# Attention and a feed-forward network on one core: pairs of units from unit 16 on, other slots for them, and the transposes' copy moved ahead of the exponentials

## The chip, the core and the metric

The kernel runs on one core of a Trainium2 chip. TensorE multiplies matrices into PSUM, VectorE and ScalarE do elementwise work, GpSimd a little more, and SP issues nearly all transfers. The metric is device time of one launch in microseconds; lower is better. The time before is 655.12 us, the median of 3 runs (654.51 to 655.52).

## The reference

Banded attention with a few global keys, then a two-layer network on its output.

```
scores = q @ k^T / sqrt(D);  rel = i - j;  keep = (j < 8) | ((rel >= 0) & (rel < 96))
bias   = -slope[h] * (96 where the key is global and not local, else |rel|)
a      = softmax(where(keep, scores + bias, -1e9));  x = a @ v        # float32
h = x @ w_in;  g = max(0.01 * h, h);  out = g @ w_out
batch 4, heads 8, seq 768, head_dim 64; 3072 tokens, d_model 512, d_ff 2048
```

The weights come as 64-bit floats. The kernel splits each weight and each activation of the network into a high and a low part and forms three of the four products.

## The kernel before

**Units and events.** A unit is one block of 128 queries and four heads; there are 24 blocks with two units each, 0 to 47. A unit passes through three events. In `event(t)` (L345), unit t gets its scores on TensorE (L181), its bias and row minimum on VectorE (`biased`, L195), its exponentials on ScalarE (`exps`, L210) and the reciprocals of its sums (`sums`). Unit t-1 is transposed, and unit t-2 is multiplied with its values (`attn_v`, L314 and L326); the result goes to `xh` on ScalarE (L339) and `xl` on VectorE (L343), the input of the network.

**Two ways to transpose.** Units below `BY_DVE` = 14 are transposed by TensorE: `transposes` (L274) multiplies the exponentials by a diagonal of reciprocals that GpSimd forms (`dg`, L245), and ScalarE copies the result out of PSUM (`keep_pt`, L289), in `event` as the last step but the `x` copies of the lead. Units from 14 on are scaled (L237) and transposed in 32x32 blocks (L240) by VectorE; `move` then writes them to device memory (`via`, L220) and reads them back in four transfers (`pt`, L222).

**Tall units.** `tall(u)` holds for units below 14 that are not in the first block of a sequence. Their near values are laid out so that one matmul contracts over all 128 rows (L326, 8 matmuls of 128x64), where others use 16 matmuls on quarters of the array. The layout of the values in memory (`layout`) follows the same test.

**The lead and the slots.** The eight events 0 to 7 (`LEAD` = 6, `LEAD + 2` events) come first, without the network. Then the network runs in 128 slots. Chunks have 3 blocks, so 384 tokens and six units; a slot does one sixteenth of the hidden layer for one chunk: 12 matmuls into `ps_h` (`ffn1`, L797 to L799), and 9 matmuls of the slot before it into the output (`ffn2`, L818 to L820). The order is: 7 slots of chunk 0 (0 to 6), the 16 of chunk 1 (7 to 22), the other 9 of chunk 0 (23 to 31), then chunks 2 to 7 with 16 slots each (chunk 2 from slot 32). In a slot the events of that slot come first, then `ffn1` of the slot, then `ffn2` of the one before. After a chunk's last `ffn2` its three output tiles are copied out of PSUM (L466, L468) and sent.

**Conversions.** The weights come in 32 pieces (`w_in` and `w_out` in turn). A conversion of one has a scaling on ScalarE (L560), three integer steps on VectorE (L563, L565, L569), a cast on ScalarE (L573) and a subtraction on VectorE (L576). The cast and the subtraction wait in the list `due` for the next `end()` or event. Slot f needs piece 2f, and the slot after it piece 2f+1. Each conversion also issues the load of a later piece. `conv_at` gives the pieces of a slot; conversion 7 runs between event 7 and slot 0.

**Pairs.** From unit `PAIRS` = 22 on, `visit(t)` takes two units at once: `attn_v` of t-2 and t-1, scores of t and t+1, loads, bias. The exponentials of t are done there. Those of t+1, and both `sums` (scaling, transposing and moving), are put in the list `behind`, of which each slot takes one entry at `end()` and one at `more()`, two places inside `ffn1`:

```
behind.extend([lambda: exps(t + 1, [0]), lambda: (exps(t + 1, [1]), sums(t)), lambda: None, lambda: sums(t + 1)])
```

**Order.** TensorE's matmuls are all kept in program order. On the other engines `pin` keeps program order up to slot 22, in slots with a pair and while `behind` is not empty; elsewhere a planner places the instructions. `ev_at` says which event stands in which slot: before, events 8 to 13 in slots 1 to 6; 14 to 19 in slots 23, 25, 26, 28, 29, 31; 20 and 21 in 32 and 35; the pairs 22 and 24 in 39 and 44; then three pairs per chunk, in its slots 2, 7 and 12.

Of the kernel before, what the change touches and what calls it, by code (L numbers as in the profile page):

```python
# [19 lines left out]
D = 64  # L20
NU = 2
BY_DVE = 14
PAIRS = 22
TB = 32
G = 32
WIN = 96
# [3 lines left out]
CHUNKS = [3] * 8  # L30
LEAD_CONV = 7
# [16 lines left out]
def fast_path(ctx, tc, qp, kp, vp, wi, wo, nvec, weights, nmall, out, B, H, S):  # L48
    nc = tc.nc
    NB = S // P  # L50
    DM = H * D
    NK = DM // P
    NF = wi.shape[0]
# [40 lines left out]
    def load_piece(p):  # L94
        if p < len(pieces):
            m, f = pieces[p]
            t = raw.tile([P, NK * P], I64, tag="stage", name="wst", bufs=STAGES)
            pin(nc.sync.dma_start(out=t, in_=(wi, wo)[m][f].rearrange("p a b -> p (a b)")))
            staged[p] = t

    due = []

    def conversion(p):

        m, f = pieces[p]
        dh, dl = ((wih[:, :, f * P:(f + 1) * P], wil[:, :, f * P:(f + 1) * P]), (woh[:, f, :], wol[:, f, :]))[m]
        for n in range(p + 2 + (p > LEAD_CONV - 2), p + 3 + (p > LEAD_CONV - 3)):
            load_piece(n)
        scale, shift, low, *parts = split_float64(tc, pin, att, staged.pop(p), dh, dl)
        due.extend(parts)  # L110
        return scale, shift, low
# [3 lines left out]
    LEAD = NU * CHUNKS[0]  # L115

    def where(u):
        s, uu = divmod(u, NU)
        return s, uu, s % NB
# [45 lines left out]

    def tall(u):

        return u < BY_DVE and where(u)[2] > 0

    def scores(u, av):  # L170
        d = units[u]
# [28 lines left out]
    def exps(u, pairs=range(2)):  # L200
        d = units[u]
        s, uu, i = where(u)
        pr, nm = d["pr"], d["nm"]
        if "sm" not in d:
            d["sm"] = att.tile([P, 4], F32, name="sm", bufs=3)
        sm = d["sm"]
        for a in pairs:
            for j in range(2):
                p = head(u, pr, a, j)
                pin(nc.scalar.activation(out=p, in_=p, func=AF.Exp, scale=-1.0,  # L210
                                         bias=nm[:, 2 * a + j:2 * a + j + 1], accum_out=sm[:, 2 * a + j:2 * a + j + 1]))
# [67 lines left out]
    def keep_pt(u):  # L279
        d = units[u]  # L280
        if u >= BY_DVE:
            return
        s, uu, i = where(u)
        ps = d.pop("ps")
        pt = att.tile([P, 6, 2, HALF], F32, name="pt", bufs=1)
        dst = pt.rearrange("p g f q -> p f g q")
        src = ps[:, :, :6 * HALF].rearrange("p f (g q) -> p f g q", g=6)
        if i:
            pin(nc.scalar.copy(out=dst, in_=src))  # L289
        else:  # L290
            for j in range(2):
                g = slice(3 * j + 1, 3 * j + 3)
                pin(nc.scalar.copy(out=dst[:, :, g], in_=src[:, :, g]))
        d["pt"] = pt
# [43 lines left out]
    def high_x(u, av):  # L338
        pin(nc.scalar.copy(out=parts(u, 0), in_=av[:, :, 2 * KW:]))  # L339
# [5 lines left out]
    def event(t, conv=()):  # L345

        now, mid, old = t < NUNIT, t - 1 in units, t - 2 in units
        if t < LEAD + 2:

            av = (ps_lead if t % 2 else ps_x).tile([P, 2, 512], F32, tag="ps_av", name="ps_sc")  # L350
            scores(t, av)
            if mid and t <= LEAD:
                transposes(t - 1)
            if old:
                ov = ps_lead.tile([P, 2, 512], F32, tag="ps_ov", name="ps_ov")
                attn_v(t - 2, ov)
            if t > LEAD:

                transposes(t - 1)
        else:  # L360

            ov = av = ps_x.tile([P, 2, 512], F32, tag="ps_av", name="ps_av")
            attn_v(t - 2, ov)
            if now:
                scores(t, av)
            if mid:
                transposes(t - 1)
            high_x(t - 2, ov)
        if t + 2 < NUNIT:
            load_qk(t + 2)  # L370
        if t == 0:
            load_piece(1)
        ends = due[:]
        due.clear()
        if ends:
            ends[0]()
        scale, shift, low = conversion(conv[0]) if conv else [lambda: None] * 3
        if t + 1 < NUNIT:
            load_v(t + 1)
        scale()  # L380
        if now:
            biased(t, av)
            if t == LEAD + 1:
                high_x(t - 2, ov)
            exps(t)
        if t > LEAD:
            low_x(t - 2, ov)
        if ends:
            ends[1]()
        shift()  # L390
        if now:
            sums(t)
        low()
        if mid:
            keep_pt(t - 1)
        if old and t <= LEAD:
            high_x(t - 2, ov)
        if old and t <= LEAD:
            low_x(t - 2, ov)

# [26 lines left out]
    half = 7  # L427
# [42 lines left out]
            nc.sync.dma_start(out=out[r0:r0 + P, :], in_=ob)  # L470


    conv_at = {n: [n + LEAD_CONV + 1] for n in range(half)}
    conv_at.update(spread(range(15, 19), range(half, half + 4)))
    conv_at.update(spread(range(19, 2 * NF), range(half + 4, half + NF - 1)))
    ev_at = {}
    for c in range(1, NCHUNK):
        events = range(NU * first_step[c] + 2, NU * first_step[c + 1] + 2)
        slots = (range(1, half) if c == 1 else [23, 25, 26, 28, 29, 31] if c == 2 else [33, 35, 37, 40, 42, 44] if c == 3
                 else range((c - 1) * NF, c * NF - 2))  # L480
        if c > 3:

            events, slots = events[::2], [(c - 1) * NF + s for s in (2, 7, 12)]
        elif c == 3:
            events, slots = [20, 21, 22, 24], [2 * NF + s for s in (0, 3, 7, 12)]
        ev_at.update(spread(events, slots))

    for t in range(2):
# [10 lines left out]
                scale_bias(tc, tabs[:, 1], nbw, H, 1)  # L499
    ps_h = ctx.enter_context(tc.tile_pool(name="ps_h", bufs=1, space=bass.MemoryType.PSUM))  # L500
    ps_o = ctx.enter_context(tc.tile_pool(name="ps_o", bufs=3, space=bass.MemoryType.PSUM))

    for step in (*due, *conversion(LEAD_CONV)):
        if step in due:
            due.remove(step)
        step()
    behind = []
    for j in range(len(order) + 1):
        pinned[0] = j < half + NF or bool(behind) or any(t >= PAIRS for t in ev_at.get(j, ()))
        conv = list(conv_at.get(j, ()))  # L510
        for t in ev_at.get(j, ()):
            if t >= PAIRS:
                visit(t, behind)
# [326 lines left out]
def layout(q, k, v, wi, wo, ng, nl):  # L840
    B, H, S, _ = q.shape
    NB = S // P

    NU_ = H // 4

    ar = np.arange(P)
    near = np.stack([np.where(ar < G, ar - P, ar), np.where(ar < G, ar - P, np.where(ar < HALF, ar + HALF, ar + P))])
    start = (np.arange(NB) - 1)[:, None, None] * P
    own = np.broadcast_to(start + P + ar[:HALF], (NB, 2, HALF))
    near = np.where(ar < G, ar, np.maximum(start + near, 0))  # L850

    qp = q.reshape(B, NU_, 2, 2, NB, P, D).transpose(0, 4, 3, 6, 1, 2, 5)
    qp = np.ascontiguousarray(qp).reshape(B * NB, 2 * D, 2 * NU_, P)

    kh = k.reshape(B, NU_, 2, 2, S, D)
    kp = kh[:, :, :, :, np.concatenate([near, own], 2)]
    kp = np.ascontiguousarray(kp.transpose(0, 4, 1, 3, 7, 2, 5, 6)).reshape(B * NB, NU_, 2 * D, 2, 2, KW)

    kd = kp[BY_DVE // NU:].reshape(-1, NU_, 2 * D, 2, 2, 3, 2, TB).transpose(0, 1, 2, 3, 4, 6, 5, 7)
    kp[BY_DVE // NU:] = kd.reshape(-1, NU_, 2 * D, 2, 2, KW)  # L860

    vh = v.reshape(B, NU_, 2, 2, S, D)
    vn = vh[:, :, :, :, near.reshape(NB, 2, 2, HALF)].transpose(0, 4, 1, 2, 7, 5, 6, 3, 8).reshape(B * NB, NU_, P, 4, 2, D)
    vo = vh[:, :, :, :, own[:, 0]].transpose(0, 4, 1, 2, 5, 3, 6).reshape(B * NB, NU_, P, 1, 2, D)
    vp = np.ascontiguousarray(np.concatenate([vn, vo], 3))

    vt = vh[:, :, :, :, near].transpose(0, 4, 1, 6, 3, 2, 5, 7).reshape(B * NB, NU_, P, 4, 2, D)
    pe = [s for s in range(BY_DVE // NU) if s % NB]
    vp[pe, :, :, :4] = vt[pe]
    DM, DF = wi.shape  # L870
    NJ = DF // P
    wip = np.ascontiguousarray(wi.reshape(DM // P, P, NJ, DF // NJ).transpose(2, 1, 0, 3))
    wop = np.ascontiguousarray(wo.reshape(NJ, DF // NJ // P, P, DM).transpose(0, 2, 1, 3))
    wip, wop = wip.view(np.int64), wop.view(np.int64)
    n = np.concatenate([np.asarray(ng, np.int64).reshape(1), np.asarray(nl, np.int64).reshape(1)]).view(np.int32).reshape(1, 4)
    qt, kt = (np.ascontiguousarray(x.transpose(0, 1, 3, 2)) for x in (q, k))
    vt = np.ascontiguousarray(v.reshape(B, H, NB, P, D).transpose(0, 1, 3, 2, 4))
    return dict(qt=qt, kt=kt, vt=vt, qp=qp, kp=kp, vp=vp, wi=wip, wo=wop, ngl=n)
# [18 lines left out]
```

## Time and profile before

| | |
|---|---|
| median of 3 runs | 655.12 us (654.51 to 655.52) |
| the profiled execution | 657.56 us, its span 656.0 us |
| TensorE matmul busy | 632.2 us, 96% of the span |
| weight load, VectorE, ScalarE, GpSimd | 85%, 57%, 43%, 3% |
| mean granted TensorE clock | 0.99 |
| chain that ended last | TensorE 89%, VectorE 6%, ScalarE 2% |
| moved by DMA | 88.04 MB |

In the profile a row of the timeline has the start in us from the span's beginning, the duration, the engine, the source line, the operation, output and inputs, shapes and a count; in brackets stands how long the engine was idle before it and what released it. PE is TensorE, PEld its weight load, DVE VectorE, ACT ScalarE, POOL GpSimd, SPq the queue of SP. A row of the windows has a stretch, its length, the busy time and instruction count of each engine asked for, the granted clock of TensorE, the share of DMA and the rate in GB/s. Matmuls overlap, so the distance between the starts of two rows says more than the durations.

### The profile page before, as it was taken

What the parts mean: (1) busy time and instruction counts of PE and PEld (TensorE: products, weight loads), DVE (VectorE), ACT (ScalarE), POOL (GpSimd) and SP (SyncE); (2) the same over time, 40 slices, a digit from 0 to 9 for tenths busy, and PEclk for the clock granted to TensorE, in tenths of its full rate; (3) what the DMA queues carried; (4) which work ended last, traced back from release to release, by engine and by line L of the source; (5) the groups of instructions that cost most, each with busy time, mean ns of one, the idle gap of its engine ahead of it and who ended that gap; (6) DMA issues with size and microseconds to landing.
All of it is one profiled execution on the core that took longest, in us unless ns stands there. A gap on an engine that the chain in (4) does not pass through costs nothing.

```text
span 656.0 us, 14356 instructions
## 1 busy us (share of the span) xinstructions
PE 632.2 (96%) x5644; PEld 558.4 (85%) x5644; DVE 374.4 (57%) x1121; ACT 283.0 (43%) x796; POOL 21.9 (3%) x48
## 2 busy tenths in 40 slices
PE   5679999999999999999999999999999999999996
PEld 4568898988888888988989889889889889999985
DVE  6987778897667454654644645635645546232222
ACT  6976664555444342452443432443433524232221
POOL 3202210000000000000000000000000000000000
PEclk9898999999999999999999999999999999999998
DMA  8984444432766433443444444335343432010001
GB/s 278 348 305 148 163 164 144 139 97 95 217 208 224 137 85 113 142 153 112 162 129 138 148 129 122 126 106 175 121 137 131 153 118 90 8 49 1 0 1 52
DMA packets 55162, 88.04 MB, mean 134 GB/s; under 512 B 9776, under 2 KB 30256, under 8 KB 55088
## 3 DMA queue, kind: packets, MB, share of 16 engines
q1 hardware_dynamic: 55088, 87.06, 40.6%
q8 instruction: 46, 0.75, 0.5%
q14 instruction: 28, 0.23, 0.1%
HBM read 67.90 MB, written 19.14 MB: 133 GB/s over the span
## 4 chain that ended last, share of the span: by engine, by line
PE 89%; DVE 6%; ACT 2%; issue 1%; POOL 1%; DMA 0%; ACTq 0%; POOLq 0%; DVEq 0%
PE ps_h L797 14%; PE ps_o L820 13%; PE ps_h L798 13%; PE ps_h L799 13%; PE ps_o L818 13%; PE ps_o L819 13%; PE ps_v L181 2%; PE ps_v L326 2%; PE ps_av L181 1%; PE ps_v L314 1%; DVE w L569 1%; PE ps_av L326 1%; DVE w L565 1%; PE ps_tr L274 1%; PE ps_av L314 1%
## 5 line engine op out<-in xcount | busy, mean ns | idle before, releaser
L797 PE MATMUL ps_h<-xh,wih 128*128 128x384 f32 x512 | 175.8, 343 | 0.1
L798 PE MATMUL ps_h<-xl,wih 128*128 128x384 f32 x512 | 172.5, 337 | 0.0
L799 PE MATMUL ps_h<-xh,wil 128*128 128x384 f32 x512 | 172.3, 337 | 0.0
L802 DVE SCALAR_TENSOR_TENSOR t<-t 128x384 f32<-128x384 f32 x128 | 73.1, 571 | 144.7 <-ACT t L801 142.7
L801 ACT COPY t<-ps_h 128x384 f32<-128x384 f32 x128 | 61.3, 479 | 214.5 <-PE ps_h L799 214.5
L820 PE MATMUL ps_o<-woh,gl 128*128 128x512 f32 x384 | 152.1, 396 | 0.1
L818 PE MATMUL ps_o<-woh,gh 128*128 128x512 f32 x384 | 151.2, 394 | 1.0 <-ACT part L468 0.7
L819 PE MATMUL ps_o<-wol,gh 128*128 128x512 f32 x384 | 151.3, 394 | 0.0
L797 PEld LDWEIGHTS ps_h<-xh,wih 128*128 128x128 f32 x512 | 96.3, 188 | 10.3 <-ACT xh L339 3.1
L808 DVE TENSOR_TENSOR gl<-t,gh 128x384 fp32r<-128x384 f32 x128 | 71.3, 557 | 55.5 <-ACT gh L807 55.5
L798 PEld LDWEIGHTS ps_h<-xl,wih 128*128 128x128 f32 x512 | 96.3, 188 | 4.2
L799 PEld LDWEIGHTS ps_h<-xh,wil 128*128 128x128 f32 x512 | 96.2, 188 | 0.0
L807 ACT CAST gh<-t 128x384 fp32r<-128x384 f32 x128 | 65.5, 512 | 59.5 <-DVE t L802 58.7
L820 PEld LDWEIGHTS ps_o<-woh,gl 128*128 128x128 f32 x384 | 72.3, 188 | 18.0 <-DVE gl L808 2.2
L210 ACT ACTIVATE pr<-pr,nmall 128x192 f32<-128x192 f32 (+1 forms) x192 | 83.5, 438 | 3.6 <-DVE nmall L195 3.0
L818 PEld LDWEIGHTS ps_o<-woh,gh 128*128 128x128 f32 x384 | 72.2, 188 | 13.0 <-ACT part L468 1.2
L819 PEld LDWEIGHTS ps_o<-wol,gh 128*128 128x128 f32 x384 | 72.2, 188 | 11.2
L195 DVE CUSTOM_DVE_ANT_0 pr<-ps_v,nbw 128x192 f32<-128x192 f32 x88 | 25.3, 354 | 26.4 <-ACT xh L339 26.4
L210 ACT ACTIVATION_READ_ACCUMULATOR pr<-pr,nmall 128x1 f32 x192 | 36.4, 190 | 0.0
L237 DVE TENSOR_SCALAR pr<-pr,rs 128x192 f32<-128x192 f32 (+1 forms) x136 | 33.8, 312 | 1.0
L240 DVE STREAM_TRANSPOSE pr<-pr 128x768 f32<-128x768 f32 (+1 forms) x34 | 32.1, 945 | 0.9
L339 ACT CAST xh<-ps_v 128x256 fp32r<-128x256 f32 x28 | 10.5, 373 | 37.9 <-PE ps_v L181 36.2
(94 smaller groups left out, 462.7 us busy)
## 6 DMA issues: line engine op xcount, KB each, us to landing
kr<-in_kp_dram SPq DMA_DIRECT2D x40, 384.0 KB, 4.4
vr<-in_vp_dram SPq DMA_DIRECT2D x40, 320.0 KB, 4.5
via<-pr SPq DMA_DIRECT2D x30, 384.0 KB, 2.5
pt<-via SPq DMA_DIRECT2D x120, 96.0 KB, 2.3
wst<-in_wi_dram SPq DMA_DIRECT2D x16, 512.0 KB, 4.5
wst<-in_wo_dram SPq DMA_DIRECT2D x16, 512.0 KB, 3.9
qs<-in_qp_dram SPq DMA_DIRECT2D x24, 256.0 KB, 3.2
out_dram<-part SPq DMA_DIRECT2D x21, 256.0 KB, 2.1
```

The lines of the kernel that those rows point to most:

```text
L210: pin(nc.scalar.activation(out=p, in_=p, func=AF.Exp, scale=-1.0, bias=nm[:, 2 * a + j:2 * a + j + 1], accum_out=sm[:, 2 * a + j:2 * a + j ...
L237: pin(nc.vector.tensor_scalar(out=p, in0=p, scalar1=rs[:, n:n + 1], scalar2=1.0, op0=ALU.mult, op1=ALU.mult))
L797: tc.keep_in_program_order(nc.tensor.matmul(ps, lhsT=wih[:, k, fs], rhs=xh[:, k, :CT], start=(k == 0), stop=False))
L798: tc.keep_in_program_order(nc.tensor.matmul(ps, lhsT=wih[:, k, fs], rhs=xl[:, k, :CT], start=False, stop=False))
L799: tc.keep_in_program_order(nc.tensor.matmul(ps, lhsT=wil[:, k, fs], rhs=xh[:, k, :CT], start=False, stop=(k == NK - 1)))
L801: pin(copy(out=t, in_=ps))
L802: pin(nc.vector.scalar_tensor_tensor(out=t, in0=t, scalar=0.01, in1=t, op0=ALU.mult, op1=ALU.max))
L807: pin(copy(out=gh, in_=t))
L808: pin(nc.vector.tensor_tensor(out=gl, in0=t, in1=gh.bitcast(F32), op=ALU.subtract))
L818: tc.keep_in_program_order(nc.tensor.matmul(o, lhsT=gh[:, ts_], rhs=woh[:, f, :], start=first, stop=False))
L819: tc.keep_in_program_order(nc.tensor.matmul(o, lhsT=gh[:, ts_], rhs=wol[:, f, :], start=False, stop=False))
L820: tc.keep_in_program_order(nc.tensor.matmul(o, lhsT=gl[:, ts_], rhs=woh[:, f, :], start=False, stop=last))
```

## The change

- `PAIRS` falls from 22 to 16, so units 16 to 21 go through `visit`.
- Events 14 to 19 stand in slots 24, 26, 28, 30: 14 and 15 alone, 16 and 18 as pairs. Chunk 3's events become the pairs 20, 22 and 24 in slots 34, 39 and 44.
- `tall` holds only below unit `LEAD` = 6. Units 6, 7, 8, 9, 10 and 11 lose it (12 and 13 never had it); the layout of the values follows.
- From event 8 on, `keep_pt(t - 1)` comes after the bias and ahead of the exponentials.
- The conversion of piece 7 ahead of slot 0 is taken out. Slots 0 to 6 now have pieces 7; 8; 9; 10 and 11; 12; 13; 14 in place of 8 to 14. What was due is done inside slot 0.

```diff
-PAIRS = 22
+PAIRS = 16
...
     def tall(u):
 
-        return u < BY_DVE and where(u)[2] > 0
+        return u < LEAD and where(u)[2] > 0
...
             biased(t, av)
             if t == LEAD + 1:
                 high_x(t - 2, ov)
+            if mid and t >= LEAD + 2:
+
+                keep_pt(t - 1)
             exps(t)
...
         low()
-        if mid:
-            keep_pt(t - 1)
         if old and t <= LEAD:
             high_x(t - 2, ov)
+        if mid and t < LEAD + 2:
+            keep_pt(t - 1)
...
-    conv_at = {n: [n + LEAD_CONV + 1] for n in range(half)}
+    conv_at = {0: [7], 1: [8], 2: [9], 3: [10, 11], 4: [12], 5: [13], 6: [14]}
...
-        if c > 3:
+        if c > 2:
 
             events, slots = events[::2], [(c - 1) * NF + s for s in (2, 7, 12)]
-        elif c == 3:
-            events, slots = [20, 21, 22, 24], [2 * NF + s for s in (0, 3, 7, 12)]
+        elif c == 2:
+            events, slots = [14, 15, 16, 18], [24, 26, 28, 30]
...
-
-    for step in (*due, *conversion(LEAD_CONV)):
-        if step in due:
-            due.remove(step)
-        step()
     behind = []
...
-    pe = [s for s in range(BY_DVE // NU) if s % NB]
+    pe = [s for s in range(CHUNKS[0]) if s % NB]
```

## The prediction

> **What bounds the kernel now.** I read the windows by stage first, then TensorE's instructions in order of time, then the other engines and the DMA queue at the places where TensorE is late. TensorE works in program order and, from slot 2 on, almost without a gap, so a wait in its queue is lost outright, and time is saved only by less TensorE work or by a gap closed.
>
> ```profile
> core 0 of [0], span 656.0 us
> ...
> 64.00:80.00 16.00, 16.00 (x237) 13.23 (x236) 13.30 (x41) 11.53 (x32) 5.46 (x11) 1.00 0.58 191
> ```
>
> The window (columns: length, busy time of TensorE, of its weight load, of VectorE, ScalarE, GpSimd, then the granted clock) shows TensorE busy for all 16.00 us and VectorE for 13.30.
>
> The largest gap stands in slot 2. TensorE's rows, with the idle time in brackets:
>
> ```profile
> 45.56 0.40 PE L820 MATMUL ps_o<-woh,gl 128*128 128x512 f32 x1
> 49.50 0.70 PE L314 MATMUL ps_av<-pt,vr 64*64 64x128 f32 x8 [3.54 <-ACT pt L289]
> ...
> 59.00 0.45 PE L314 MATMUL ps_av<-pt,vr 64*64 64x128 f32 x8
> ...
> 60.04 0.88 PE L181 MATMUL ps_av<-kr,qs 64*64 64x192 f32 x16
> 60.74 0.88 PE L274 MATMUL ps_tr<-dg,pr 64*64 64x64 f32 x48
> ...
> 63.74 0.39 PE L818 MATMUL ps_o<-woh,gh 128*128 128x512 f32 x1
> ...
> 65.90 0.45 PE L314 MATMUL ps_av<-pt,vr 64*64 64x128 f32 x8
> ```
>
> The rows at 49.50, 59.00 and 65.90 open events 9, 10 and 11. TensorE was free at 45.56 + 0.40 = 45.96 and waited 3.54 us for ScalarE's copy of unit 7's transposes (L289). Event 9 with its slot then took 59.00 - 49.50 = 9.50 us, event 10 with its slot 6.90. The granted clock (third figure of a row) explains the excess of 2.60 us:
>
> ```profile
> 48.00:50.00 2.00, 0.50 (x8) 0.64 0.79 309
> 50.00:52.00 2.00, 2.00 (x32) 0.50 0.04 12
> ```
>
> So this gap costs 3.54 + 2.60 = 6.14 us. Why the copy was late is read on VectorE, ScalarE and GpSimd:
>
> ```profile
> 38.33 0.66 DVE L569 SCALAR_TENSOR_TENSOR w<-wst,w 128x512 int32<-128x512 int32 x1
> ...
> 39.67 0.69 DVE L576 TENSOR_TENSOR wil<-w,wih 128x512 fp32r<-128x512 f32 x1 [0.69 <-ACT wih L573]
> ...
> 40.28 0.42 DVE L563 TENSOR_SCALAR w<-w 128x512 int32<-128x512 int32 x1
> ...
> 41.47 0.69 DVE L569 SCALAR_TENSOR_TENSOR w<-wst,w 128x512 int32<-128x512 int32 x1
> ...
> 45.72 0.35 DVE L195 CUSTOM_DVE_ANT_0 pr<-ps_av,nbw 128x192 f32<-128x192 f32 x1
> 45.83 0.62 ACT L573 CAST wih<-w 128x512 fp32r<-128x512 f32 x1 [1.76 <-DVE w L569]
> ...
> 46.36 0.66 ACT L560 ACTIVATE w<-wst 128x512 f32<-128x512 f32 x1
> ...
> 46.92 0.44 ACT L210 ACTIVATE pr<-pr,nmall 128x192 f32<-128x192 f32 x1
> ...
> 48.67 0.78 ACT L289 COPY pt<-ps_tr 128x768 f32<-128x768 f32 x1
> ...
> 49.42 0.88 POOL L245 TENSOR_TENSOR dg<-eye,rs 128x256 f32<-128x256 f32 x1 [9.96 <-DVE rs L231]
> ```
>
> VectorE goes through the low words of conversion 6 (ends 38.99), conversion 7 (40.28 to 42.16) and conversion 8, so that event 8's bias starts only at 45.72, when TensorE has nearly finished all that stands behind event 8 in its queue (45.96). Event 8's exponentials follow at 46.92 and, behind all four, the copy at 48.67.
>
> **The change, part by part.**
>
> *Conversion 7 moves from ahead of slot 0 into it, 8 and 9 a slot later, and 11 joins 10 in slot 3.* One conversion fewer stands before event 8's bias. Starting from the end of conversion 6's low word at 38.99, VectorE has slot 0's three FFN and weight operations (0.57, 0.69 and 0.56; the row at 39.67 has the second, the page's groups below the others) with short waits on ScalarE between them, until about 41.2, then conversion 7's 1.88 until about 43.1. Bias 8 starts there instead of 45.72. ScalarE then has conversion 7's cast (0.62), conversion 8's scaling (0.66, as at 46.36) and, now ahead of the exponentials, the copy (0.78), which ends near 45.1: before 45.96, so TensorE does not wait for it.
>
> ```profile
> L802 DVE SCALAR_TENSOR_TENSOR t<-t 128x384 f32<-128x384 f32 x128 | 73.1, 571 | 144.7 <-ACT t L801 142.7
> ...
> L808 DVE TENSOR_TENSOR gl<-t,gh 128x384 fp32r<-128x384 f32 x128 | 71.3, 557 | 55.5 <-ACT gh L807 55.5
> ```
>
> *The copy ahead of the exponentials (events 8 to 14).* The exponentials of event 8 start at about 45.1 and end, by the 48.67 - 46.92 = 1.75 of the traced ones, at 46.85. The sums, and GpSimd's 0.88 at L245, make the transposes' right side ready at about 48.1. TensorE reaches those transposes at 45.96 + 1.04 + 0.70 (rows 59.00 to 60.74), less the 0.3 of the next part: 47.4. That is a new wait of 0.7. Bounds: 0 and 3.1 (the whole gap stays to half, as if ScalarE's 0.78 and one 1.88 of VectorE stood in it again). I take 0.7, which comes from rows of this slot. Gain: 6.14 - 0.7 = 5.4 us. Queued behind the copy on ScalarE are the exponentials and the FFN copy t. From event 10 on, the transposes are wanted 6.9 us after the scores, and copy plus exponentials plus GpSimd are 0.78 + 1.75 + 0.88, so nothing is late there. Slot 3's second conversion is 1.88 + 0.69 on VectorE; what hides it is the 16.00 - 13.30 = 2.70 us per 16 that VectorE has free and the 3 us by which the copy now runs ahead of its reader; uncovered it would cost up to 1.9. I take nothing. The loads that these conversions issue on SP move behind event 8's query and key loads; each is read two slots later at the earliest, and TensorE is not behind SP at that place.
>
> *Units 6 to 11 lose the tall form.* Their near values go back to quarter-array matmuls, twice as many. From event start to scores the tall form took 60.04 - 59.00 = 1.04 us; the other form, in a later event:
>
> ```profile
> 165.75 0.45 PE L314 MATMUL ps_av<-pt,vr 64*64 64x128 f32 x8
> ...
> 171.24 0.45 PE L314 MATMUL ps_av<-pt,vr 64*64 64x128 f32 x8
> ...
> 171.98 0.83 PE L181 MATMUL ps_av<-kr,qs 64*64 64x192 f32 x16
> ...
> 181.23 0.45 PE L314 MATMUL ps_av<-pt,vr 64*64 64x128 f32 x8
> ...
> 187.07 0.45 PE L314 MATMUL ps_av<-pt,vr 64*64 64x128 f32 x8
> ```
>
> 171.98 - 171.24 = 0.74, so 0.30 for each of six units: 1.8 us gained. The transposes are as many as before, and the copy has the same shape. Bounds: 0 and 1.8 (the end of a pipelined stretch is read from the next one's start).
>
> *Event 14 leaves slot 23, where chunk 1 ends.* The first matmuls into fresh output buffers, in slot 24:
>
> ```profile
> 162.44 0.40 PE L818 MATMUL ps_o<-woh,gh 128*128 128x512 f32 x1
> ...
> 164.85 0.50 PE L818 MATMUL ps_o<-woh,gh 128*128 128x512 f32 x1 [0.72 <-ACT part L468]
> ```
>
> Six matmuls lie between these rows, but 2.41 us; nine take 65.90 - 63.74 = 2.16, so six 1.44. The wait, for ScalarE's copy of a finished output part behind event 14's exponentials, is 0.97. In the changed kernel slot 23 has no event, and event 14's matmuls stand between the end of chunk 1 and that first use. I take 1.0 gained; bounds 0 and 1.0.
>
> *Units 16 to 21 go in pairs.* From the event rows above, one slot with its event is 187.07 - 181.23 = 5.84, two slots with one are 9.99: a slot is 4.15 and a single event 1.69 (the one at 165.75, of a block with little near work, 5.49 - 4.15 = 1.34). A pair, with five slots to the next:
>
> ```profile
> 235.60 0.45 PE L314 MATMUL ps_v<-pt,vr 64*64 64x128 f32 x8
> ...
> 237.02 1.51 PE L181 MATMUL ps_v<-kr,qs 64*64 64x192 f32 x32
> ...
> 259.49 0.45 PE L314 MATMUL ps_v<-pt,vr 64*64 64x128 f32 x8
> ```
>
> 23.89 - 5 x 4.15 = 3.14, against 2 x 1.69 = 3.38: 0.24 for each of three pairs, 0.7 gained.
>
> *But the pairs stand too close.* A unit from 14 on is transposed on VectorE, sent out to memory and fetched back (via, pt), and the pair at t multiplies units t-2 and t-1 with its first matmuls. The old list left three slots between a unit's event and its reader, and five behind a pair. The new one, 14 at slot 24, 15 at 26, 16/17 at 28, 18/19 at 30, leaves two. The fetches (SP's rows: issue, duration of the four issues), and the page's time from issue to landing, 2.3:
>
> ```profile
> 176.64 1.75 SPq L222 DMA_DIRECT2D pt<-via  x4
> 181.32 1.73 SPq L222 DMA_DIRECT2D pt<-via  x4
> ...
> 248.02 2.69 SPq L222 DMA_DIRECT2D pt<-via  x4
> ...
> 253.48 1.73 SPq L222 DMA_DIRECT2D pt<-via  x4
> ```
> ```profile
> via<-pr SPq DMA_DIRECT2D x30, 384.0 KB, 2.5
> pt<-via SPq DMA_DIRECT2D x120, 96.0 KB, 2.3
> ```
>
> Unit 15 has landed 176.64 + 1.75 + 2.3 - 165.75 = 14.9 us after its event began, unit 16 by its rows 14.1. The pair in slot 28 wants unit 15 after 1.34 + 8.30 + 0.74 (unit 14's own multiplication) = 10.4. Wait A: 3.7 to 4.6, I take 4.15.
>
> The pair in slot 30 follows its predecessor by 3.14 + 8.30 = 11.44. The first unit of a pair lands 248.02 + 2.69 + 2.3 - 235.60 = 17.4 after the pair began, a wait of 6.0; its multiplication takes 0.74 (18.15), and the second lands 253.48 + 1.73 + 2.3 - 235.60 = 21.9, a wait of 3.8. Wait B: 9.7. VectorE's transpose of the second unit,
>
> ```profile
> 248.66 0.98 DVE L240 STREAM_TRANSPOSE pr<-pr 128x768 f32<-128x768 f32 x1
> ```
>
> ends at 249.64, and with 2.5 out (the page's median for via), 1.73 and 2.3 it would land at 20.6 if SP were never busy: B is then 8.4, the lower bound.
>
> The pair in slot 34 comes four slots behind. From the scores' start (237.02) the second unit lands 257.51 - 237.02 = 20.5 later, and TensorE asks after 1.72 + 16.6 + 0.74 = 19.06. Wait C: 1.4, lower bound 0.
>
> Queued behind these waits on TensorE is everything: scores of the pair, the FFN, and through it all other engines. SP's fetches do not wait for the stalled pair, as they belong to units before it.
>
> A and B are longer than the 3.54 us behind which the clock stood at 0.50, so each brings the 2.60 again, measured in the same kind of work (bounds 0 and 2.6 for A, 2.6 for B). [...]
>
> Sum: gains 5.4 + 1.8 + 1.0 + 0.7 = 8.9; losses 4.15 + 2.6 + 9.7 + 2.6 + 1.4 = 20.45. Net +11.55. The profiled execution took 657.56 us (span 656.0), so 669.1; it stands 2.44 above the median of the runs, 655.12, on which the forecast is 666.7.
>
> **The rivals.**
>
> 1. *Faster: the relay through memory is quick enough for slot 30.* If unit 17 landed within 12.2 us of its pair's beginning instead of 21.9, B and C with B's clock drop fall away, and 655.12 - 8.9 + 6.75 = 653.0. It decides from where B and its drop cost less than 8.9 - 6.75 = 2.15, a landing before about 14.3. For it: ScalarE, busy 11.53 of 16.00 us even in the window quoted first, could run the exponentials earlier. Against: in a pair the second unit's sums are written behind the next slot's FFN work, which puts VectorE's transpose alone at 13.1 after the beginning (248.66). 0.13, with the case that A is hidden too (646.2) in it.
> 2. *The first gap comes back.* The copy is early, but the exponentials behind it, or slot 3's two conversions, hold up TensorE as long as before. For it: VectorE has only 2.7 us in 16 free. Against: the walk above leaves 0.7. Then 666.7 + 5.4 = 672.1. 0.13.
> 3. *Only B bites.* Unit 15's fetch lands in time, since the singles' work is not held to program order in slots 24 to 27. Against: its rows are themselves from such slots. 666.7 - 6.75 = 660.0. 0.10.
> 4. *No net effect*, waits shorter throughout so that they balance the gains: 655. 0.04.
>
> **How the numbers follow.** The forecast has 0.60. Its own range: gains at most 6.14 + 3.5 = 9.6 with losses at least 3.7 + 8.4 + 2.6 = 14.7 give 655.12 + 5.1 = 660.2; losses of 4.6 + 2.6 + 9.7 + 2.6 + 1.4 = 20.9 with gains of only 3.0 (half the first gap) and 0.7 give 672.3. Of all cases, 0.60 + 0.13 + 0.10 = 0.83 are slower by over 0.2% (1.3 us, about what a measurement of this kernel tells from no change), 0.13 faster, 0.04 the same. The range 657.5 to 673 holds the forecast, case 2 and case 3.
>
> **What would show it.** Right: no TensorE gap over 1 us in slot 2 and the clock at 1.00 through 48 to 64 us; event 14 without a wait for a part's copy in slot 24; TensorE idle in the pairs of slots 28 and 30 with the fetch of pt as releaser, some 4 and 10 us, and a granted clock of 0.50 behind each. Wrong: no idle time at the pairs' first matmuls, or these waits ended by another engine; a gap of 3 us or more in slots 1 to 6.

## The result, and the profile after

The changed kernel takes 665.05 us (median of 3, 664.79 to 667.25) against 655.12: a ratio of 1.0149, 95% interval 1.0112 to 1.0186. The forecast was 666.7 (657.5 to 673), slower. Its profiled execution took 664.79 us with a span of 663.3.

TensorE's waits of the changed kernel, grouped (total us, times, longest):

```profile
PE ps_v L314 <- DMA pt<-via: 9.5, 6, 3.8
```

The kernel before has no such row. The windows (length, busy time of TensorE, weight load, VectorE, ScalarE, GpSimd, granted clock) show where they lie:

```profile
144.00:176.00 32.00, 29.65 (x267) 25.87 (x265) 17.48 (x51) 13.05 (x37) 0.00 (x0) 1.00 0.37 120
176.00:208.00 32.00, 24.85 (x252) 21.10 (x251) 14.10 (x58) 11.34 (x42) 0.00 (x0) 0.79 0.49 157
```

From 144 to 208 us TensorE is idle for 2.35 + 7.15 = 9.5 us, and from 176 to 208 us its clock is 0.79. Both places are pairs. TensorE's rows from slot 28 to slot 34:

```profile
172.52 0.45 PE L314 MATMUL ps_v<-pt,vr 64*64 64x128 f32 x8
...
175.78 0.40 PE L314 MATMUL ps_v<-pt,vr 64*64 64x128 f32 x2 [2.35 <-DMA pt<-via]
176.89 0.48 PE L314 MATMUL ps_v<-pt,vr 64*64 64x128 f32 x3 [0.71 <-DMA pt<-via]
...
180.46 0.44 PE L795 MATMUL ps_h<-xh,wih 128*128 128x384 f32 x1
...
192.82 0.40 PE L314 MATMUL ps_v<-pt,vr 64*64 64x128 f32 x2 [3.80 <-DMA pt<-via]
193.68 0.48 PE L314 MATMUL ps_v<-pt,vr 64*64 64x128 f32 x3 [0.45 <-DMA pt<-via]
...
197.14 0.66 PE L314 MATMUL ps_v<-pt,vr 64*64 64x128 f32 x2 [1.91 <-DMA pt<-via]
198.07 0.49 PE L314 MATMUL ps_v<-pt,vr 64*64 64x128 f32 x3 [0.28 <-DMA pt<-via]
...
202.12 0.69 PE L795 MATMUL ps_h<-xh,wih 128*128 128x384 f32 x1
...
219.75 0.45 PE L314 MATMUL ps_v<-pt,vr 64*64 64x128 f32 x8
```

The pair in slot 28 begins at 172.52 and gives TensorE to the FFN at 180.46, after 7.94 us; the same stretch of the pair at 235.60 in the kernel before is 2.86:

```profile
238.46 0.44 PE L797 MATMUL ps_h<-xh,wih 128*128 128x384 f32 x1
```

The pair in slot 28 costs 5.08 more: 3.06 idle, the rest work at the lower clock (0.63 from 176 to 178 us, 0.52 from 178 to 180). From 172.52 to the pair in slot 34 (219.75) pass 47.23 us; two pairs and six slots at 3.14 and 4.15 would be 31.18. Of the 16.05 in excess, 5.08 belong to slot 28 and 10.97 to the pair in slot 30; slot 34 has no wait. The clock of TensorE (third figure) at both:

```profile
178.00:180.00 2.00, 2.00 (x40) 0.52 0.00 0
...
200.00:202.00 2.00, 2.00 (x27) 0.50 0.10 19
```

The first slots, in the rows that open events 8 to 11 and the one that waits:

```profile
39.13 0.45 PE L314 MATMUL ps_av<-pt,vr 64*64 64x128 f32 x8
...
45.67 0.45 PE L314 MATMUL ps_av<-pt,vr 64*64 64x128 f32 x8
...
48.64 0.93 PE L274 MATMUL ps_tr<-dg,pr 64*64 64x64 f32 x48 [1.40 <-POOL dg L245]
...
53.90 0.45 PE L314 MATMUL ps_av<-pt,vr 64*64 64x128 f32 x8
...
60.44 0.45 PE L314 MATMUL ps_av<-pt,vr 64*64 64x128 f32 x8
```

The 3.54 us gap in front of event 9 is gone, and so is the slow clock (1.00 from 36 to 64 us). From event 8 to event 10 it takes 14.77 us; before it was 59.00 - 38.82 = 20.18. In its place stands a wait of 1.40 for GpSimd's right side of the transposes, the diagonal of reciprocals that they are multiplied with. In slot 24 no output part is waited for. Slot 28 begins at 172.52, against 181.23 before, where one event more (1.69) had been done by then: 7.0 us ahead. The changed kernel is then behind by 8.3 at the pair of unit 22, which begins at 243.86 against 235.60.

### The profile page after: what moved, and what is told of

The parts are those of the page before. It is cut to its first block, busy times and chain, and to the rows that moved or that the text cites. A ratio compares the mean times of both kernels' runs of the same rounds, so it can differ in the third digit from the quotient of the medians.

```text
span 663.3 us, 14539 instructions
## 1 busy us (share of the span) xinstructions
PE 633.5 (96%) x5740; PEld 562.1 (85%) x5740; DVE 376.2 (57%) x1121; ACT 282.7 (43%) x796; POOL 22.2 (3%) x48
## 4 chain that ended last, share of the span: by engine, by line
PE 85%; DVE 4%; DMA 4%; ACT 4%; issue 1%; SPq 1%; POOL 0%; POOLq 0%; DVEq 0%; ACTq 0%
PE ps_h L795 13%; PE ps_h L797 12%; PE ps_h L796 12%; PE ps_o L818 12%; PE ps_o L817 12%; PE ps_o L816 12%; PE ps_v L181 3%; PE ps_v L326 2%; DMA kr<-in_kp_dram 2%; PE ps_v L314 2%; ACT pr L210 1%; DMA via<-pr 1%; PE ps_sc L181 1%; DVE w L567 1%; DMA pt<-via 1%
## 5 line engine op out<-in xcount | busy, mean ns | idle before, releaser
L195 DVE CUSTOM_DVE_ANT_0 pr<-ps_v,nbw 128x192 f32<-128x192 f32 x112 | 32.3, 353 | 46.2 <-ACT xh L339 46.1
L339 ACT CAST xh<-ps_v 128x256 fp32r<-128x256 f32 x34 | 12.7, 373 | 62.5 <-PE ps_v L181 60.8
```

## The experiments

Theory D (distance) says that the loss is the waits of pairs whose units began two slots earlier, and that the rest of the change gains. Rivals: that the pair form itself costs; that the early gain is lost again. For the early gain, theory V says that VectorE's conversion held up the copy, theory S that the copy's place did. Line numbers in the rows shift a little from kernel to kernel; the operation and the tile tell what is meant. Ratios are to the kernel before, run on the same chip beside them; its medians there were 655.47 us for the first four experiments, 656.51 or 656.11 for the others, and differences in us go by the ratio.

**The old pairs and slots, the rest of the change kept.**

```diff
-PAIRS = 16
+PAIRS = 22
...
-        if c > 2:
+        if c > 3:
...
-        elif c == 2:
-            events, slots = [14, 15, 16, 18], [24, 26, 28, 30]
+        elif c == 3:
+            events, slots = [20, 21, 22, 24], [2 * NF + s for s in (0, 3, 7, 12)]
```

> The changed kernel with the old pairs and the old slots of events 14 to 25; what remains of the change is the moved conversion, the copy ahead of the exponentials and the lost tall form. Theory D (distance: the loss is made of waits at the pairs whose units began only two slots earlier): those waits are gone and the gain of the first slots stays, which the trace of the changed kernel shows as 5.5 us at the start of slot 7, so 649.6 us; TensorE has no wait over 1 us for a fetch of pt. Rival: the early gain is given back later, because the events that follow are bound by something else; then about 655.

Measured: 650.10 us, ratio 0.992 (0.9901 to 0.994). No fetch of pt is waited for; in slot 24 the output part still is:

```profile
159.55 0.50 PE L816 MATMUL ps_o<-woh,gh 128*128 128x512 f32 x1 [0.70 <-ACT part L471]
```

The early gain is real and lasts to the end. The whole loss, and more, sits in the slots and pairs. In this trace there is no wait of 1.40 in event 9; TensorE is idle for 1.29 us inside event 8 instead, and the profile names no releaser for it. So the 1.40 of the changed kernel is not the same in every execution.

**The slots and pairs alone**, on the kernel before.

```diff
-PAIRS = 22
+PAIRS = 16
...
-        if c > 3:
+        if c > 2:
...
-        elif c == 3:
-            events, slots = [20, 21, 22, 24], [2 * NF + s for s in (0, 3, 7, 12)]
+        elif c == 2:
+            events, slots = [14, 15, 16, 18], [24, 26, 28, 30]
```

> The kernel before with only the pairs from unit 16 on and the new slots. Theory D: 655.1 + 5.1 (wait and slow clock at the pair in slot 28) + 11.1 (the same in slot 30) - 0.7 (three pairs) - 1.0 (slot 23) = 669.6 us. Rival: the waits come about only with the moved conversions or with the copy's new place; then 653 to 656.

Measured: 668.25 us (runs from 665.75 to 671.02), ratio 1.0214 (1.0175 to 1.0253), 14 us over the kernel before. Its rows at the pair of slot 30, and its first gap, which is still there:

```profile
48.95 0.45 PE L314 MATMUL ps_av<-pt,vr 64*64 64x128 f32 x8 [3.55 <-ACT pt L289]
...
195.57 0.40 PE L314 MATMUL ps_v<-pt,vr 64*64 64x128 f32 x2 [3.99 <-DMA pt<-via]
```

Within the spread of the runs the two halves add up: -5.2 (0.992) and +14.0 (1.0214) make +8.8, and the whole change measures +9.9. The waits need neither the moved conversions nor the copy's new place.

**Wider slots**, on the changed kernel.

```diff
-            events, slots = [14, 15, 16, 18], [24, 26, 28, 30]
+            events, slots = [14, 15, 16, 18], [24, 25, 28, 31]
```

> The changed kernel with events 14, 15, 16, 18 in slots 24, 25, 28, 31 in place of 24, 26, 28, 30: every unit is three slots or more away from its reader. Theory D: the wait in slot 28 goes with its slow clock (5.1 us), that of the next pair becomes one slot (4.15 us) shorter, so about 655.8 us, or 653 if the clock then stays up. Rival (the pair form itself is what costs, by its fixed order or its shared PSUM tile): 664 to 666 as before this edit.

Measured: 662.98 us, ratio 1.0112 (1.009 to 1.0134), hardly faster than the change, and so far from the 655.8 of theory D. The time alone would speak for the rival; the rows do not:

```profile
173.25 0.45 PE L314 MATMUL ps_v<-pt,vr 64*64 64x128 f32 x8
...
192.87 0.40 PE L314 MATMUL ps_v<-pt,vr 64*64 64x128 f32 x2 [2.56 <-DMA pt<-via]
193.97 0.49 PE L314 MATMUL ps_v<-pt,vr 64*64 64x128 f32 x3 [0.71 <-DMA pt<-via]
...
217.17 0.66 PE L314 MATMUL ps_v<-pt,vr 64*64 64x128 f32 x2 [5.12 <-DMA pt<-via]
218.24 0.48 PE L314 MATMUL ps_v<-pt,vr 64*64 64x128 f32 x3 [0.42 <-DMA pt<-via]
```

The pair in slot 28, three slots behind its second unit, waits for nothing, so the pair form does not cost by itself. The next, three slots behind that pair, waits 2.56 + 0.71 (and 0.17 before) in place of 6.44 (3.80 + 0.45 + 1.91 + 0.28). But I had overlooked that the pair in slot 34 is now three slots behind its predecessor and no longer four: it waits 5.12 + 0.42. Its units' transfers in SP's queue, and VectorE's rows, tell why it is more than in slot 31:

```profile
207.27 1.76 SPq L222 DMA_DIRECT2D pt<-via  x4
209.55 0.43 SPq L148 DMA_DIRECT2D qs<-in_qp_dram  x1
210.43 0.32 SPq L220 DMA_DIRECT2D via<-pr  x1
214.51 1.74 SPq L222 DMA_DIRECT2D pt<-via  x4
```
```profile
205.28 1.88 DVE L462 TENSOR_TENSOR kept<-ps_o,kept 128x512 f32<-128x512 f32 x3
209.43 0.97 DVE L240 STREAM_TRANSPOSE pr<-pr 128x768 f32<-128x768 f32 x1
```

The second unit's write out (via, 210.43) stands behind the fetches of the first and a load of queries, but SP was done with these at 209.98. What it waited for was VectorE's transpose, which ended at 210.40: VectorE had first to add up the output of chunk 0 (1.88), so the two transposes of this pair lie 5.56 us apart, where those of the pair before lie 4.03. The write out then took 4.08 us until the fetches behind it, against 2.74 for the pair before (190.24 - 187.50); why is not shown. So the expectation was wrong by a pair that I had not recounted, and the mechanism holds: with two slots the second unit of a pair is far behind (6.44 us of waits in the changed kernel's slot 30), with three about 3 to 5.5 us, with four 0 to 0.7 (the pair in slot 34 of the changed kernel and of the three other kernels that have it there), with five nothing.

**TensorE kept busy in the waits**, on the changed kernel: matmuls into a region that the scores overwrite.

```diff
         for u, av in zip(ts, avs):
+            for _ in range({(16, 17): 10, (18, 18): 17, (18, 19): 8}.get((t, u), 0)):
+                tc.keep_in_program_order(nc.tensor.matmul(av[:, 0, :2 * KW], lhsT=wih[:, 0, :P], rhs=wih[:, 0, :2 * KW],
+                                                          start=True, stop=True))
             attn_v(u - 2, av)
```

> The changed kernel with idle matmuls (128x384, results overwritten) on TensorE ahead of the first multiplications of the waiting units: 10 ahead of unit 15's, 17 ahead of unit 16's, 8 ahead of unit 17's. Theory: part of the loss is the half clock behind an idle TensorE; kept busy, it stays at 1.00, the pair in slot 28 costs 2.0 us less and the one in slot 30 about 2.9 less: 660.1 us. Rival: the slow rows behind the waits come from late operands, not from the clock: 665, or more by what the added matmuls take.

Measured: 662.78 us, ratio 1.0111 (1.0088 to 1.0134), 2.3 below the change, with intervals that overlap. The clock and TensorE's rows:

```profile
178.00:180.00 2.00, 2.00 (x44) 0.50 0.00 0
...
198.00:200.00 2.00, 1.50 (x53) 1.00 0.58 146
```
```profile
180.94 0.45 PE L798 MATMUL ps_h<-xh,wih 128*128 128x384 f32 x1
...
198.24 0.40 PE L314 MATMUL ps_v<-pt,vr 64*64 64x128 f32 x2 [1.37 <-DMA pt<-via]
...
201.04 0.44 PE L798 MATMUL ps_h<-xh,wih 128*128 128x384 f32 x1
...
205.29 0.34 PE L798 MATMUL ps_h<-xh,wih 128*128 128x384 f32 x1
```

In slot 30 the clock stays at 1.00. From the second unit's values to the FFN it takes 201.04 - 198.24 = 2.80 where the changed kernel takes 202.12 - 197.14 = 4.98; its FFN slot is 4.25 long, that of the changed kernel 5.04 (202.12 to 207.16). So the slow rows behind the wait come from the clock (1.00 here from 192 to 204 us, 0.50 from 194 to 202 us in the changed kernel). From the FFN behind the first pair to the FFN behind the second it takes 201.04 - 180.94 = 20.10, in the changed kernel 202.12 - 180.46 = 21.66. In slot 28 TensorE was still idle for 1.40 and 0.63 us behind the ten matmuls: the clock is 0.50 there all the same, and the gain of 2.0 expected there is missing. That pair even took 180.94 - 171.85 = 9.09 us in this trace, against 7.94. The profiled execution (665.44 us) is the longest of the four.

**Where the second unit of the pair is held up**, on the changed kernel.

```diff
-            behind.extend([lambda: exps(t + 1, [0]), lambda: (exps(t + 1, [1]), sums(t)), lambda: None, lambda: sums(t + 1)])
+            early = [lambda: exps(t + 1), lambda: (sums(t), sums(t + 1))]
+            behind.extend(early if t == 16 else [lambda: exps(t + 1, [0]), lambda: (exps(t + 1, [1]), sums(t)), lambda: None, lambda: sums(t + 1)])
```

> The changed kernel with one difference: behind the pair in slot 28, the second unit's exponentials and sums are all given to slot 28 in place of two steps in slot 28 and two in slot 29. Question: what makes unit 17's fetch the last to land before the pair in slot 30. Theory V (VectorE's place for it, one slot later): its transpose then ends 1.7 us earlier, and so does the wait, 1.7 us off the changed kernel's 665.1: 663.4. Rival Q (SP's queue: unit 17's write out is issued only after the four fetches of unit 16, at 191.87 in the changed kernel, 0.1 behind them): the write out is issued as late as before, the wait stays, 665.

Measured: 666.79 us, ratio 1.0165 (1.0144 to 1.0185). In the changed kernel SP's rows and VectorE's transpose of unit 17 were

```profile
187.65 0.33 SPq L220 DMA_DIRECT2D via<-pr  x1
190.02 1.75 SPq L222 DMA_DIRECT2D pt<-via  x4
191.87 0.38 SPq L220 DMA_DIRECT2D via<-pr  x1
194.48 1.73 SPq L222 DMA_DIRECT2D pt<-via  x4
```
```profile
190.63 0.98 DVE L240 STREAM_TRANSPOSE pr<-pr 128x768 f32<-128x768 f32 x1
```

and here

```profile
191.63 0.33 SPq L220 DMA_DIRECT2D via<-pr  x1
193.99 1.75 SPq L222 DMA_DIRECT2D pt<-via  x4
195.84 0.38 SPq L220 DMA_DIRECT2D via<-pr  x1
```
```profile
193.28 0.98 DVE L240 STREAM_TRANSPOSE pr<-pr 128x768 f32<-128x768 f32 x1
```

In the changed kernel the transpose ended at 191.61 (190.63 + 0.98) and the write out followed at 191.87, 0.1 behind the last fetch of unit 16 (190.02 + 1.75). Here the transpose ended at 194.26, but the write out was issued at 195.84, again 0.1 behind unit 16's fetches (193.99 + 1.75). The two transposes moved together from 3.99 to 2.65 us apart, and the two write outs stayed 4.2 apart. In both traces SP issued writes and fetches in the order of the program, the fetches only 2.4 to 2.6 us behind the write before them, so here the second unit was not written out earlier, although its transpose had ended 1.58 us before (195.84 - 194.26). Rival Q holds. The edit also delayed unit 16, whose sums now stand behind all of unit 17's exponentials; that fits a time above the 665 of rival Q.

**The moved conversions alone**, on the kernel before.

```diff
-    conv_at = {n: [n + LEAD_CONV + 1] for n in range(half)}
+    conv_at = {0: [7], 1: [8], 2: [9], 3: [10, 11], 4: [12], 5: [13], 6: [14]}
...
-    for step in (*due, *conversion(LEAD_CONV)):
-        if step in due:
-            due.remove(step)
-        step()
```

> The kernel before with the moved conversions alone (pieces 7; 8; 9; 10, 11; 12; 13; 14 in slots 0 to 6, none ahead of slot 0); the copy stays behind the exponentials. Theory V (VectorE's conversion 7 is what held the copy up): event 8's bias comes 2.6 us earlier, its four exponentials end near 46.2, the copy near 47.0, so TensorE waits about 1.2 us in slot 2 in place of 3.54, the clock stays at 1.00, and the later wait for the transposes' right side (1.40 in the changed kernel) is gone: 655.3 - 4.9 = 650.4 us. Rival S (the copy's place behind the exponentials is what counts): the gap stays at 2.5 us or more, and the clock still drops: 653 or more.

Measured: 653.13 us, ratio 0.995 (0.9932 to 0.9969), 3.3 us faster. The row at event 9:

```profile
48.17 0.45 PE L314 MATMUL ps_av<-pt,vr 64*64 64x128 f32 x8 [0.93 <-ACT pt L289]
```

The wait is 0.93, the clock stays at 1.00 (from 40 to 62 us) and no transpose waits later: theory V in its mechanism. The time by itself would also fit rival S (653 or more); the rows rule it out. From event 8 to event 13 the trace takes 75.71 - 40.22 = 35.49 us, the kernel before 79.56 - 38.82 = 40.74, so 5.25 less in these slots. The medians show 3.3 where 4.9 was expected; a part of the reason is shown two experiments on.

**The copy ahead of the exponentials alone**, on the kernel before.

```diff
             biased(t, av)
+            if mid and t >= LEAD + 2:
+                keep_pt(t - 1)
             exps(t)
...
-        if mid:
+        if mid and t < LEAD + 2:
             keep_pt(t - 1)
```

> The kernel before with the copy ahead of the exponentials from event 8 on, and nothing else. Theory V: event 8's bias still starts near 45.7; the copy ends near 47.65, a wait of 1.7 in slot 2, and the exponentials end 0.8 later, so that TensorE waits another 1.35 for the transposes' right side; the two are too short for the clock to drop: 655.3 - 3.1 = 652.2 us. Rival S: the whole gap goes: 649 to 650. Rival N: the second wait eats what the first gives, and the clock drops as before: 655.

Measured: 654.36 us, ratio 0.9974 (0.9952 to 0.9995).

```profile
46.75 0.45 PE L314 MATMUL ps_av<-pt,vr 64*64 64x128 f32 x8 [1.81 <-ACT pt L289]
...
50.05 1.56 PE L274 MATMUL ps_tr<-dg,pr 64*64 64x64 f32 x48 [0.70 <-POOL dg L245]
```
```profile
48.00:50.00 2.00, 1.35 (x16) 0.50 0.53 202
```

Two waits of 1.81 and 0.70 stand in place of 3.54; the first is as walked through (1.7), the second is half of the 1.35 expected. The clock fell to 0.50 all the same in the profiled execution, and it did so behind the first wait: it is 0.96 from 46 to 48 us and 0.50 from 48.00 on, and the second wait lies at 49.35 to 50.05. So theory V's condition, two waits too short for the clock to drop, failed. The gain is 1.7 us, between what V and N expected; theory S is out, as most of the gap is left.

**The form of units 6 to 11 alone**, on the kernel before.

```diff
-        return u < BY_DVE and where(u)[2] > 0
+        return u < LEAD and where(u)[2] > 0
...
-    pe = [s for s in range(BY_DVE // NU) if s % NB]
+    pe = [s for s in range(CHUNKS[0]) if s % NB]
```

> The kernel before with units 6 to 11 in the form without tall matmuls (and the layout of the values that goes with it), nothing else. Theory: 0.30 to 0.36 us less TensorE work in each of the five events that are not swallowed by the gap of slot 2: 655.3 - 1.7 = 653.6 us. Rival: the shorter events bring nothing, since the copy and the transposes' right side then come as late as before: 655.

Measured: 654.42 us, ratio 0.9972 (0.9952 to 0.9993), 1.8 us faster, as expected, with 0.5 to 3.1 in the interval. The rows are surer: from event 10 to event 11, and from there to event 12, it takes 6.54 in place of 6.90 and 6.91. The profile has an unlooked-for row:

```profile
50.85 0.45 PE L314 MATMUL ps_av<-pt,vr 64*64 64x128 f32 x8 [3.17 <-ACT pt L289]
```
```profile
50.00:52.00 2.00, 1.15 (x52) 1.00 0.51 199
```

The gap in front of event 9 is 3.17 us, and the clock behind it is 1.00. In the kernel before, the clock behind its 3.54 us was 0.50. The kernel with the slots and pairs alone runs the same code as the kernel before up to slot 22, and there event 9 with its slot took 57.46 - 48.95 = 8.51 behind a gap of 3.55: 1.61 over 6.90, where the kernel before lost 2.60. So three profiles give 3.2, 5.2 and 6.1 us for nearly the same gap, and what closing it gains, on average, can be less than the 6.14 read from one of them. That fits the 3.3 us of the moved conversions; that it explains all of the missing 1.6 is not shown.

**Single units up to 19, three slots to each reader.**

```diff
-PAIRS = 16
+PAIRS = 20
...
-        if c > 2:
+        if c > 3:
 
             events, slots = events[::2], [(c - 1) * NF + s for s in (2, 7, 12)]
+        elif c == 3:
+            events, slots = [20, 22, 24], [35, 40, 45]
         elif c == 2:
-            events, slots = [14, 15, 16, 18], [24, 26, 28, 30]
+            slots = [24, 25, 27, 28, 30, 31]
```

> The changed kernel with single units up to 19 in slots 24, 25, 27, 28, 30, 31 and pairs 20, 22, 24 in slots 35, 40, 45: every single unit three slots or more from its reader, every pair five, and no event in slot 23. Theory D: no wait for a fetch anywhere; against the kernel with the old slots (650.1) the wait of 0.7 in slot 24 goes and one pair more saves 0.25: 649.0 us. Rival: an event in slots 24 and 25 or 27 and 28, one right behind the other, makes a new wait for a copy or an output part: 650 to 652.

Measured: 649.15 us, ratio 0.9892 (0.9855 to 0.9929). The window from slot 22 on (length, TensorE busy, clock, DMA share, rate):

```profile
144.00:208.00 64.00, 64.00 (x594) 1.00 0.56 180
```

TensorE is busy throughout, in this window and up to 288 us, no event waits for a fetch or for an output part, and the clock is 1.00. This beats both kernels. Against the old slots (0.992, 0.9901 to 0.994) the intervals overlap; that the wait in slot 24 is gone is read from the rows.

**The same with the copy back behind the exponentials.**

```diff
-            if mid and t >= LEAD + 2:
-                keep_pt(t - 1)
             exps(t)
...
-        if mid and t < LEAD + 2:
+        if mid:
             keep_pt(t - 1)
```

> The kernel with three slots between single units and their readers (649.15, e8), with the transposes' copy back behind the exponentials; the moved conversions stay. Theory: with the conversions moved, the copy's new place costs more than it brings: the waits for the transposes' right side (1.39 and 0.80) go, and a wait for the copy of 0.93, as with the conversions alone, comes in their place: 1.3 us faster, 647.9, ratio to the kernel before 0.987. Rival: the copy ahead is worth something beside these waits; then 650 or more.

Measured: 649.08 us, ratio 0.9887 (0.9867 to 0.9906). The waits are as expected in kind, one of 1.34 for the copy and none for the transposes' right side:

```profile
48.21 0.45 PE L314 MATMUL ps_av<-pt,vr 64*64 64x128 f32 x8 [1.34 <-ACT pt L289]
```

The time cannot be told from that of the kernel with the copy ahead, so the runs do not show the 1.3 us expected. The traces do, in these slots alone: from event 8 to event 13 it takes 74.28 - 40.26 = 34.02 us here and 73.75 - 38.53 = 35.22 with the copy ahead. This profile reached event 8 only at 40.26, 1.7 later than the other, although the code up to there is the same in both.

**One conversion in each of slots 0 to 6**, copy ahead.

```diff
-    conv_at = {0: [7], 1: [8], 2: [9], 3: [10, 11], 4: [12], 5: [13], 6: [14]}
-    conv_at.update(spread(range(15, 19), range(half, half + 4)))
-    conv_at.update(spread(range(19, 2 * NF), range(half + 4, half + NF - 1)))
+    conv_at = {n: [n + LEAD_CONV] for n in range(half)}
+    conv_at.update(spread(range(14, 2 * NF), range(half, half + NF - 1)))
```

> The kernel with three slots between single units and their readers (649.15, e8), with one conversion in each of slots 0 to 6 (7 to 13), and 14 to 31 spread over slots 7 to 21. Theory: the wait of 0.80 in slot 5 comes from slot 3's two conversions on VectorE and goes; the rest stays: 648.3. Rival: that wait stays, since it belongs to the copy ahead of the exponentials; or slots 7 to 21, which have one conversion more, get later: 649.2 to 650.

Measured: 649.98 us, ratio 0.9918 (0.9896 to 0.994). The wait of 0.8 in event 12 is gone here, and it was gone with the copy back, so it came from slot 3's two conversions together with the copy ahead. But slot 8 has a new one, for ScalarE's copies of chunk 0's first half:

```profile
86.20 0.50 PE L817 MATMUL ps_o<-woh,gh 128*128 128x512 f32 x1 [1.77 <-ACT kept L458]
```

It takes back what the other gave.

## Why the prediction was right, point by point

**The close places of the pairs: right, and each term too large.** Wait A was put at 4.15 with 2.6 for the clock; the trace has 5.08 in all, 3.06 of it idle. The first matmul of unit 15 reads only the rows of the first two of its four fetches and ran inside the wait. Wait B was put at 9.7 with 2.6; the trace has 10.97. Of these only 6.44 are idle time, because the slow clock (0.50 from 194 us on) also stretched the first unit's multiplication (from 193.68 to 195.23, where 0.74 was reckoned) while the second unit was under way. With the clock kept up, the stretch between the two pairs' FFNs took 20.10 where 11.44 would do (a pair and two slots): 8.66 for the wait alone, and 21.66 - 20.10 + 5.04 - 4.25 = 2.35 for the clock. Counted from the FFN's first matmul behind the pair, unit 17 landed after 194.48 + 1.73 + 2.3 - 180.46 = 18.05 us, where the rows used had 257.51 - 238.46 = 19.05. The step that was mis-sized is the four fetches at 248.02: their issue took 2.69 in that row and 1.75 here, and the second unit's write out followed only 0.1 behind them (at 250.81 in the kernel before, at 191.87 here). Wait C was put at 1.4 and is 0 in the changed kernel. Sum of the losses: 20.45 forecast, 16.05 in the trace.

**The first gap: right in kind, too large.** The copy is early, as walked through, and event 9 starts at 45.67 where 45.96 was said. The wait for the transposes' right side is 1.40 and not 0.7: the right side is ready at 48.6 and not at 48.1, and TensorE asks for it 0.2 earlier. The step "I take nothing" for slot 3's second conversion failed: event 12 waits 0.86,

```profile
69.19 0.93 PE L274 MATMUL ps_tr<-dg,pr 64*64 64x64 f32 x48 [0.86 <-POOL dg L245]
```

and only in kernels where slot 3 has two conversions and the copy goes ahead. From event 8 to event 13 the changed kernel takes 74.40 - 39.13 = 35.27 us, before 79.56 - 38.82 = 40.74, so 5.47 less; five events without the tall form give 0.36 each of that (6.90 to 6.54), which leaves 3.7 for the conversions and the copy, where 5.4 was forecast. The gain belongs to the conversions, which alone bring 5.25 in these slots; the copy's new place, once they are moved, takes 1.2 back. The diff also puts the copy behind the `x` copies in the lead's events up to 6, which the list of changes leaves out. Event 8 begins at 39.13 and before at 38.82, closer together than executions of the same code come (37.82 to 41.00), so its effect is not shown.

**The form of units 6 to 11: right.** 1.8 forecast, 1.8 measured alone.

**Slot 23: right in kind.** The wait of 0.70 in slot 24 stands in the kernel with the old slots and not in the changed one; with what the six matmuls lose beside it, 1.0 was forecast, and no run measured that by itself.

**The pairs' smaller work** (0.7) was not measured by itself.

**The sum.** Gains until slot 28 are 7.0 against the 8.2 forecast; losses 16.05 against 20.45. In the traces the net is 8.3 at the pair of unit 22 and 663.3 - 656.0 = 7.3 at the end; in the medians it is 9.9, as the profiled execution of before lay 2.44 above its median and that of after 0.26 below. So 11.55 was too high by 1.6 in the medians: by the trace of the changed kernel the gains were over-sized by some 1 and the losses by some 4, and part of the rest is the spread between executions. Gains and losses were both over-sized, so the errors cancelled in part; that is luck. In the medians the first slots gave 5.2 where 5.4 + 1.8 = 7.2 was forecast, and the slots and pairs cost 14.0 where 20.45 - 1.0 - 0.7 = 18.75 was forecast. One step of the sum was inconsistent too: it took 2.44 off because the profiled execution stood above the median, but kept the whole 6.14 of the gap that this execution showed. Of the rivals, a relay quick enough for slot 30 is refuted by the rows, and so is "only B bites"; the first gap did not come back.

**The clock.** Behind both waits the granted clock is 0.50, as said, and keeping TensorE busy in one of them kept it up (1.00 from 192 to 204 us). It cost 2.0 behind the first wait (5.08 - 3.06) and 2.35 at the second, where 2.60 was taken for each.

## What to carry to other kernels

When steps of a pipeline are merged or moved, count for each consumer how far its producer now is in time, and compare that with the traced latency of the whole path, with every queue it passes: here about 14 us for a unit alone and 21 for the second of a pair, against 10.4 and 12.2. Recount all consumers after each move, since a wait that is shortened in one place is easily moved to the next (in the wider slots, to slot 34 with 5.12 + 0.42 us). Where a path goes through one queue, here SP's, look at what the second unit really waits for. In slot 28's pair the queue held it up, and starting it earlier on VectorE gained nothing; in the wider slots it was VectorE itself.

## What the runs showed of the hardware

In these runs the drop of TensorE's clock did not follow the length of the gap alone. It fell to 0.50 about 1.2 us behind a single wait of 1.81 us (the copy alone), and stayed at 1.00 behind an unbroken one of 3.17 (the form alone). I had taken every gap of 3.5 us or more to cost 2.6 us; behind 3.54 and 3.55 us, in two kernels with the same code up to there, it cost 2.60 and 1.61. Counted from the granted clock of the windows of 2 us (twice each window's length times what its clock lacks to 1.00), the clock was at 0.50 for 3.40 us in slot 28 of the changed kernel and 3.44 in slot 2 of the slots and pairs alone, for 6.80 in slot 2 of the kernel before and 6.84 in that of the copy alone, and for 10.24 in slot 30 of the changed kernel: in these five places close to a whole multiple of 3.4. No fixed length of a gap decides in these runs; what does is not shown.

The lead is where executions differ. Drops to 0.50 fall there at other places in each profile: from 16 to 22 us in the kernel before, from 18 to 28 in the changed one. The kernel with one conversion in each of slots 0 to 6 has a mean granted clock of 0.998 over its span, where these two have 0.99 and 0.983, and its 48 transposes of one event take 0.93 us at 21.40, 29.52 and 34.54, where the changed kernel has 1.56 at 21.98 under a clock of 0.50. The changed kernel and seven of its variants, with the same code up to event 8, reach it between 37.82 and 41.00 us. So a difference of 1 or 2 us between two profiles is read from the slots in question, and not from their spans.
